# Seven block products in the first product of chunk 0, and two blocks of W2 converted during the attention

## The chip, the cores and the metric

One core of one Trainium2 chip runs the whole program. Time is the device time of one execution in microseconds (us). In this text TensorE makes matrix products and transposes, VectorE, ScalarE and GpSimd (POOL) work on elements, and SP (SyncE) issues the DMA transfers.

## The reference

```python
def reference(**kwargs):
    ...
    attn_out = _attn_ref(**attn_kwargs)      # sliding window of 64, (4, 8, 576, 64)
    x = np.ascontiguousarray(attn_out.transpose(0, 2, 1, 3)).reshape(B, S, H * D)
    x = _moe_ref(x=x, **moe_kwargs)
    return _moe2_ref(x=x, **moe2_kwargs)

def _moe_ref(x, w_in, w_spatial, b_spatial, w_out):
    h = np.maximum(x @ w_in, 0.0)
    u, v = (h[..., :512], h[..., 512:])
    ...                                      # v_n: v normalised over its last axis
    v_s = np.einsum('ts,bsd->btd', w_spatial, v_n) + b_spatial[None, :, None]
    return ((u * v_s) @ w_out)

def _moe2_ref(x, w_tok1, w_tok2, w_ch1, w_ch2):
    h = np.maximum(x.transpose(0, 2, 1) @ w_tok1, 0.0) @ w_tok2
    u = x + h.transpose(0, 2, 1)
    h2 = np.maximum(u @ w_ch1, 0.0) @ w_ch2  # 512 -> 1536 -> 512
    return (u + h2)
```

There are 4 x 576 = 2304 tokens of 512 features. The weights come as float64. In what follows W1 is `w_ch1` and W2 is `w_ch2`.

## The kernel before

Every large product is made of three matmuls: each factor is split into a rounded high part and a low part (h and l at the end of a name), and high x high, high x low and low x high are added (`mm3`, line 161). A split is a cast on ScalarE (line 148) and a subtraction on VectorE or POOL (line 149). A float64 weight is first made float32 out of its two 32-bit words: `down` on ScalarE (line 72), then `to_f32` on VectorE (lines 63, 68, 69). This whole step is called a conversion below.

The program has three stages. The first is the attention with the first half of the MoE block. It runs in 18 turns whose instructions are in an order written out by hand (`manual_schedule`, lines 463 to 565). A turn n transposes the softmax of turn n (line 285), takes the exponentials of turn n+1 (line 264) and their norm (`rs`, lines 272 to 274), and makes the scores and the maximum of turn n+2 (lines 241 and 255). Between them run pieces of the MoE block's products as work to fill TensorE, among them the spatial product, whose PSUM bank VectorE empties in lines 394 and 395. SP loads q and k (`qq`, `kk`) three turns ahead and v (`va`, `vb`) two turns ahead. All transfers of the kernel stand in SP's one queue, in program order.

The second stage makes, per piece, `wout` (the product with w_out), `x2nat` (transposes), `tok1` and `tok2` (the two products over tokens), and beside them converts the weights of the channel MLP. `load_c1(j)`, j = 0 to 5, converts two column tiles of W1, splits them, forms four sums of their blocks on POOL and stores these to DRAM (`sums`, line 717). `load_c2(j)` converts two row tiles of W2, forms block sums on POOL (line 738), splits all eight blocks (the low part on POOL, line 149) and stores them to DRAM (`scr`, line 742). Here the order on each engine is a list scheduler's; the conversions are given a later priority (`later`, LATER). Their raw words, their float32 values and their high and low parts live in a ring of eight buffers of 4 KB a partition (`k4`). `tok1` splits its result with `hl` on VectorE (line 672); `tok2` needs that `hl`.

The third stage goes over the tokens in three chunks of 768. The first product of a chunk (512 to 1536) goes over six block rows j. Chunk 0 makes it plainly: `ch1` (line 819) for column tiles j and j+6. Chunks 1 and 2 make it by `ch1_seven` (line 838): a two-by-two block product with seven products in place of eight. That needs sums of the activations' blocks, t1 to t4 (`usums`, split into spare places), and the sums of W1, loaded back (`load_sums`). The second product is `product` (line 889): seven block products with weights loaded from `scr`; it is the same in all chunks.

Of the kernel before, what the change touches and what calls it, by code (L numbers as in the profile page):

```python
# [35 lines left out]
def tile_kernel(ctx, tc, qT, kT, kE, v, w_in, wsT, b_sp, w_out, w_t1, w_t2, w_c1, w_c2, outT):  # L36
# [422 lines left out]
    def wv_part(k):  # L459
        return w_part(U[:, k, 1152:2176], w_in[128 * k:128 * k + 128, 512:].unsqueeze(1), wi_h[:, k:k + 1, 512:], wi_l[:, k:k + 1, 512:], 512)  # L460

    E = mybir.EngineType
    with tc.manual_schedule(engines={E.PE, E.SP, E.Activation, E.DVE, E.Pool}):
# [61 lines left out]
        uv_v(*its[0])  # L525
        conv, late = {1: (0,), 2: (1, 2), 3: (3,)}, ()
        ws_at = {2: 2, 3: 2, 4: 3, 5: 3}
        for n in range(1, len(its)):
            more, some = n + 2 < len(its), n + 1 < len(its)
            cv = [wu[i] for i in conv.get(n, ())]  # L530
            if n > 1:
                if n + 3 < len(its):
                    load_qk(n + 3)
                if more:
                    load_v(n + 2)
            PT = att_turn(n, busy={1: 2, 2: 8}.get(n, 0))
# [12 lines left out]
            go(*cv[1:])
            att_pv(n, PT)  # L550
            go(*cv[1:])
            if more:
                scores(n + 2)
                smax(n + 2, 0)
                smax(n + 2, 1)
            if n > 1:
                tick()
            late = cv[1:]
            while work and left > 0:
                left -= run_work(1)  # L560
# [166 lines left out]
    @later  # L727
    def load_c2(j):

        X = [k4() for _ in range(2)]  # L730
        Y = [x.rearrange("p (s c) -> p s c", s=4) for x in X]
        convert(X[0])

        def blk(s, n=1):
            return Y[s // 4][:, s % 4:s % 4 + n, :]

        for o, a, b, op in ((4, 1, 3, ALU.add), (5, 4, 0, ALU.subtract), (6, 0, 1, ALU.subtract), (7, 2, 5, ALU.subtract)):
# [16 lines left out]
    def usums(c, u):  # L754

        t0 = TW * c
        (uh, ul), (vh, vl) = u
        x11, x21, x12, x22 = [U[:, k:k + 2, t0 + h:t0 + h + HW] for h in (0, HW) for k in (0, 2)]

        def thirds(t):  # L760
            return t.rearrange("p k (j c) -> p k j c", c=128)

        def apart(w, words):
            v = words.rearrange("p (j w r k c) -> p j w r k c", j=3, w=2, r=2, k=4)
            return v[:, :, w, 1, :2].rearrange("p j k c -> p k j c")
# [16 lines left out]
    tok1(0)  # L782
    load_c2(1)
    x2nat(1)
    wout(3)
    tok2(0)
    load_c2(2)
    load_c1(1)
# [16 lines left out]
    tok1(3)  # L805
    load_c2(4)
    tok2(2)
    u = [uin(0, 0)]
    load_c1(4)
    tok2(3)  # L810
# [7 lines left out]

    def ch1(u, ft):

        out = []
        for uh, ul in u:
            ps = psmm.tile([P, 512], F32, tag="mm", name="mm")[:, :HW]
# [13 lines left out]

    def ch1_seven(X):

        x11, x21, x22, t1, t2, t3, t4 = X  # L840
        S = [load_sums(j) for j in range(2)]
        outs, left = [], []
        for j in range(NJ):
            if j and j + 1 < NJ:
                S.append(load_sums(j + 1))
            s1, s2, s3, s4 = S[j]
            a, c = [psmm.tile([P, 512], F32, tag="mm", name="mm")[:, :HW] for _ in range(2)]
# [64 lines left out]
    for c in range(NTOK // TW):  # L912
        t0 = TW * c
        u = u[:1] if c == 0 else []
        u += [uin(c, h) for h in range(len(u), 2)]
        if c:
            b11, b12, b21, b22, e = ch1_seven(usums(c, u))
        else:
            b11, b12, b21, b22, e = [], [], [], [], []
            for j in range(NJ):  # L920
                if j == 0:
                    load_c1(5)
                    load_c2(5)
                x, y = ch1(u, j)
                b11.append(x)
                b12.append(y)
                x, y = ch1(u, j + NJ)
                b21.append(x)
                b22.append(y)
                e.append(diff(H(), b12[j], b11[j], nc.vector))  # L930
                diff(b12[j], b22[j], b12[j], nc.vector)
        us = [[U[:, 2 * dh:2 * dh + 2, t0 + HW * h:t0 + HW * h + HW] for h in range(2)] for dh in range(2)]
# [119 lines left out]
```

## Time and profile before

| | |
|---|---|
| median of 3 runs | 638.13 us (638.07 to 638.38) |
| profiled execution, its own time | 638.47 us |
| its span | 636.7 us |
| TensorE busy | 610.3 us, 96%, 4455 matmuls and transposes |
| VectorE busy | 459.5 us, 72% |
| ScalarE busy | 334.1 us, 52% |
| POOL busy | 153.4 us, 24% |
| TensorE's granted clock | 1.00 over nearly the whole span |
| DMA | 103.60 MB, mean 163 GB/s |

The profile is of one execution; the span is from its first to its last instruction, and the program's own time is a little longer. The attention ends near 215 us. The stage of wout, tok1 and tok2 runs to 363.5, chunk 0 from there to about 500 (its first product to 412), and chunks 1 and 2 follow, each started a little before the one ahead of it ends. A line of a timeline gives start, busy time, engine, source line and tiles; in square brackets stands the idle time of the engine just before it and what ended it.

### The profile page before, as it was taken

Reading aid. Unit: us, or ns where it says so; the run is one execution under the profiler, and the core shown is the slowest. Engines: PE = TensorE matmul, PEld = TensorE weight load, DVE = VectorE, ACT = ScalarE, POOL = GpSimd, SP = SyncE. Lnnn points to the kernel's source line nnn. Section 1 sums busy time; section 2 is a strip of 40 time slices with the busy share of each in tenths; the row PEclk is TensorE's granted clock in tenths of the full one; section 3 lists DMA queues with packets and bytes.
Section 4 is the critical chain, followed back from the end, with each engine's and each line's share of the span. In section 5 each row is a group of like instructions: output and inputs, shape, how many; then the busy total and the mean of one; then the engine's idle time right before and its main releaser. Section 6 shows DMA issues by size and latency. Waiting matters only on the chain.

```text
span 636.7 us, 12004 instructions
## 1 busy us (share of the span) xinstructions
PE 610.3 (96%) x4455; PEld 566.8 (89%) x4455; DVE 459.5 (72%) x977; ACT 334.1 (52%) x839; POOL 153.4 (24%) x166
## 2 busy tenths in 40 slices
PE   5889999999999999999899999999999999999997
PEld 2568798998889899888788899999999999999987
DVE  4896857556584688769978951278875998867982
ACT  4777853545674464666554442345543646344550
POOL 5610000100010010565475471041000440002510
PEclk9999999999999999999999999999999999999999
DMA  8853473222330135557756455057433675534772
GB/s 325 271 158 112 152 235 127 78 77 75 102 116 2 34 118 158 177 193 248 256 183 218 183 174 218 0 198 257 149 125 133 220 230 196 178 103 151 255 248 75
DMA packets 46106, 103.60 MB, mean 163 GB/s; under 512 B 4192, under 2 KB 16736, under 8 KB 46048
## 3 DMA queue, kind: packets, MB, share of 16 engines
q1 hardware_dynamic: 46048, 102.84, 48.3%
q8 instruction: 35, 0.57, 0.4%
q14 instruction: 23, 0.19, 0.1%
HBM read 83.95 MB, written 18.87 MB: 162 GB/s over the span
## 4 chain that ended last, share of the span: by engine, by line
PE 64%; DVE 14%; ACT 7%; DMA 5%; issue 4%; POOL 3%; SPq 1%; DVEq 0%; ACTq 0%; POOLq 0%
PE mm L161 27%; PE A L904 17%; PE mm L833 8%; PE A L833 6%; ACT pb L264 3%; DMA U<-in_w_in 3%; POOL k L738 2%; DVE k L68 2%; DVE k L69 2%; PE xo L297 2%; PE pt L285 2%; DMA scr<-hl 2%; DVE k L63 1%; PE A L161 1%; PE sc L241 1%
## 5 line engine op out<-in xcount | busy, mean ns | idle before, releaser
L904 PE MATMUL A<-oh,w 128*128 128x384 f32 x480 | 102.7, 334 | 0.0
L886 POOL TENSOR_TENSOR H<-H 128x384 f32<-128x384 f32 x36 | 45.0, 1264 | 184.9 <-DVE ol L899 171.0
L899 DVE TENSOR_TENSOR ol<-H,oh 128x384 fp32r<-128x384 f32 x120 | 77.2, 676 | 16.4 <-ACT oh L898 12.7
L904 PEld LDWEIGHTS A<-oh,w 128*128 128x128 f32 x480 | 85.0, 188 | 0.0
L898 ACT CAST oh<-H 128x384 fp32r<-128x384 f32 x120 | 60.0, 514 | 41.5 <-PE A L904 31.0
L904 PE MATMUL A<-ol,w 128*128 128x384 f32 x240 | 61.4, 336 | 2.2 <-DVE ol L899 2.2
L161 PE MATMUL mm<-ws,nh 128*128 128x288 f32 x320 | 62.0, 297 | 0.4 <-DVE tmp L394 0.4
L161 PEld LDWEIGHTS mm<-ws,nh 128*128 128x128 f32 x320 | 49.9, 188 | 1.0 <-DVE tmp L394 0.6
L363 POOL TENSOR_SCALAR rstd<-mv 128x1 f32<-128x1 f32 x18 | 4.9, 272 | 178.4 <-DVE mv L362 178.3
L904 PEld LDWEIGHTS A<-ol,w 128*128 128x128 f32 x240 | 43.1, 188 | 3.3 <-DVE ol L899 3.2
L886 DVE TENSOR_TENSOR H<-H 128x384 f32<-128x384 f32 x36 | 22.6, 628 | 21.8 <-ACT H L826 19.6
L161 PE MATMUL mm<-ws,nl 128*128 128x288 f32 x128 | 37.7, 295 | 0.0
L264 ACT ACTIVATE pb<-pb,nm 128x128 f32<-128x128 f32 x96 | 37.3, 400 | 0.4 <-DVE nm L255 0.4
L286 ACT COPY PT<-pt 128x512 f32<-128x512 f32 x36 | 19.4, 591 | 31.5 <-PE pt L285 31.5
L272 DVE TENSOR_SCALAR rs<-sm 128x8 f32<-128x8 f32 (+1 forms) x19 | 3.3, 172 | 42.9 <-ACT pb L264 42.9
L161 PE MATMUL mm<-xh,wi_h 128*128 128x384 f32 x96 | 32.7, 341 | 0.7 <-ACT vf L357 0.6
L161 PE MATMUL mm<-xh,wi_l 128*128 128x384 f32 x96 | 32.1, 334 | 0.0
L161 PE MATMUL mm<-xl,wi_h 128*128 128x384 f32 x96 | 32.1, 334 | 0.0
L161 PE MATMUL mm<-gh,wo_h 128*128 128x512 f32 (+1 forms) x80 | 29.4, 378 | 0.1
L161 PE MATMUL mm<-gh,wo_l 128*128 128x512 f32 (+1 forms) x80 | 29.4, 370 | 0.0
L161 PE MATMUL mm<-gl,wo_h 128*128 128x512 f32 (+1 forms) x80 | 29.4, 370 | 0.0
L149 POOL TENSOR_TENSOR hl<-k,hl 128x512 fp32r<-128x512 f32 (+1 forms) x24 | 28.6, 1208 | 0.0
(190 smaller groups left out, 1691.4 us busy)
## 6 DMA issues: line engine op xcount, KB each, us to landing
w<-scr SPq DMA_DIRECT2D x63, 512.0 KB, 4.4
k<-in_w_c SPq DMA_DIRECT2D x24, 512.0 KB, 5.3
scr<-hl SPq DMA_DIRECT2D x18, 512.0 KB, 6.1
kk<-in_kT SPq DMA_DIRECT2D x16, 384.0 KB, 4.7
k<-sums SPq DMA_DIRECT2D x12, 512.0 KB, 3.2
qq<-in_qT SPq DMA_DIRECT2D x18, 256.0 KB, 4.0
va<-in_v SPq DMA_DIRECT2D x18, 256.0 KB, 2.9
vb<-in_v SPq DMA_DIRECT2D x18, 256.0 KB, 3.9
```

What stands on the lines that cost most here:

```text
L68: nc.vector.scalar_tensor_tensor(out=y, in0=high, scalar=-0x80000000, in1=y, op0=ALU.bitwise_and, op1=ALU.bitwise_or)
L69: nc.vector.scalar_tensor_tensor(out=y, in0=low, scalar=29, in1=y, op0=ALU.logical_shift_right, op1=ALU.bitwise_or)
L149: eng.tensor_tensor(out=lo, in0=x, in1=f(hi), op=ALU.subtract)
L161: nc.tensor.matmul(o, a, c, start=(i == 0), stop=(i == n - 1))
L264: nc.scalar.activation(out=pb[:, h, :], in_=scs[g][:, h - 4 * g, :] if mk is None else pb[:, h, :], func=AF.Exp, scale=SCALE if mk is None ...
L285: nc.tensor.transpose(pt[:, h, :], pb[:, 4 * g + h, :], ident)
L286: nc.scalar.copy(out=PT[:, 4 * g:4 * g + 4, :], in_=pt)
L833: nc.tensor.matmul(o, a, m, start=first and i == 0, stop=i == len(todo) - 1, skip_group_check=True)
L886: eng.tensor_tensor(out=out, in0=a, in1=b, op=ALU.subtract)
L898: nc.scalar.copy(out=oh, in_=blk[j])
L899: nc.vector.tensor_tensor(out=ol, in0=blk[j], in1=f(oh), op=ALU.subtract)
L904: nc.tensor.matmul(acc[d], a, m, start=(first and j == 0 and i == 0), stop=(last and j == NJ - 1 and i == 2), skip_group_check=True)
```

## The change

In the first product of chunk 0 only block rows 0 and 1 are made plainly; rows 3, 4, 5 and 2, in that order, are made by seven block products as in the other chunks. So t1 to t4 and the sums of W1 are needed for chunk 0 too, and `usums` gives them in two steps, one after the first plain row and one after the second, into other spare places. And W2's blocks j = 0 and 1 are converted during the attention by `early_c2`, in the same manner as `load_c2` but with the four sums and the low parts on VectorE and in free columns of the tile U: block 0 in turns 2 to 6, block 1 in turns 6 to 10. Each is a generator whose steps (load, downs, to_f32, sums, casts, subtractions, stores) are called at one of three points of a turn: before the exponentials ("exp"), after the scores ("mid"), and at the end ("end"). The other ten conversions keep their functions; their order of loads changes, and load_c2(4) and (5) are called in the two plain rows.

```diff
+    def early_c2(j):
...
+        for r, src in zip(raw, c2_source(j)):
+            nc.sync.dma_start(out=r, in_=src.bitcast(I32))
...
+        yield
+        for i, (low, high) in enumerate(parts):
+            down(span(2, 2 * i, 2), high)
+        yield
+        to_f32(span(2, 0, 4), parts)
+        yield
+        for o, a, b, op in C2_SUMS:
+            nc.vector.tensor_tensor(out=val[o], in0=val[a], in1=val[b], op=op)
+        yield
+        homes = ((2, 2, 0, 0, 2), (4, 2, 0, 2, 2), (6, 2, 1, 0, 2), (0, 1, 1, 2, 1))
+        for s, n, r, at, w in homes:
+            nc.scalar.copy(out=span(r, at, n).bitcast(F32R), in_=span(2 + s // 4, s % 4, n))
+        yield
+        for s, n, r, at, w in homes:
+            x = span(2 + s // 4, s % 4, n)
+            nc.vector.tensor_tensor(out=x.bitcast(F32R), in0=x, in1=span(r, at, n), op=ALU.subtract)
+        yield
+        for h, blocks in ((0, ((2, 4, 0, 0), (6, 2, 1, 0), (0, 1, 1, 2))), (1, ((4, 4, 3, 0), (2, 2, 2, 2), (0, 1, 2, 0)))):
+            for s, n, r, at in blocks:
+                nc.sync.dma_start(out=scr[s:s + n, j // 2, :, j % 2, h].rearrange("s p c -> p s c"), in_=span(r, at, n).rearrange("p (s c) -> p s c", c=256))
...
+        EARLY, FROM = 2, 2
+        side = [early_c2(j) for j in range(EARLY)]
+        at = {(FROM + 4 * j + t, point): side[j] for j in range(EARLY)
+              for t, point in ((0, "end"), (1, "mid"), (2, "exp"), (3, "exp"), (3, "mid"), (4, "exp"), (4, "mid"))}
...
-                ((2, 0), (1, 0), (2, 1), (2, 2), (1, 1), (1, 2), (2, 3), (1, 3), (2, 4), (1, 4), (1, 5), (2, 5))]
+                ((1, 0), (2, 2), (1, 1), (1, 2), (2, 3), (1, 3), (1, 4), (1, 5), (2, 4), (2, 5))]
...
-        for i, o, a, b in ((0, t1, x12, x11), (1, t2, x22, t1), (2, t3, x22, x12), (3, t4, x21, t2)):
+        for i, o, a, b in ((0, t1, x12, x11), (1, t2, x22, t1)):
             nc.vector.tensor_tensor(out=o, in0=a, in1=b, op=ALU.subtract)
             split(*homes[i], thirds(o))
...
+        yield
+        for i, o, a, b in ((2, t3, x22, x12), (3, t4, x21, t2)):
+            nc.vector.tensor_tensor(out=o, in0=a, in1=b, op=ALU.subtract)
+            split(*homes[i], thirds(o))
...
+    def ch1_all(u, parts, plain):
+
+        outs, left = {}, []
+        seven_js = [j for j in (*range(NJ // 2, NJ), *range(NJ // 2))] if plain else list(range(NJ))
+        seven_js = [j for j in seven_js if j >= plain]
+        for j in range(plain):
+            if j < 2:
+                load_c2(4 + j)
+            outs[j] = ch1_four(u, j)
+            if j == 0:
+                next(parts)
...
+        S = {j: load_sums(j) for j in seven_js[:2]}
+        x11, x21, x22, t1, t2, t3, t4 = next(parts)
+        for at, j in enumerate(seven_js):
+            if at and at + 1 < len(seven_js):
+                S[seven_js[at + 1]] = load_sums(seven_js[at + 1])
+            s1, s2, s3, s4 = S.pop(j)
...
+        b11, b12, b21, b22, e = ch1_all(u, usums(c, u), 0 if c else 2)
```

Three places where the order moves. The first is SP's queue at the end of turn 6 and the start of turn 7; this is a piece of the difference. The first two rows end the loads of v for turn 8, the last two are q and k of turn 10.

```order
 L215 DMA va<-in_v 128x512
 L216 DMA vb<-in_v 128x512
+L508 DMA scr<-U 128x4x256
+L508 DMA scr<-U 128x2x256
+L508 DMA scr<-U 128x256
+L508 DMA scr<-U 128x4x256
+L508 DMA scr<-U 128x2x256
+L508 DMA scr<-U 128x256
+L486 DMA U<-in_w_c 128x1024 x2
 L200 DMA qq<-in_qT 128x512
 L203 DMA kk<-in_kT 128x768
```

Six stores of block 0 and two loads of block 1 now stand between the two. Behind `kk` come three raw pieces of w_out (line 85), as before.

The second place is VectorE near the end of the second stage, around the two `hl` of tok1(1). Before (the conversion with k4_4303 is c1(3)):

```order
L149 TENSOR_TENSOR ul_4459<-U_83,uh_4458 128x768 x2
L335 TENSOR_TENSOR nl_4042<-A_4036,nh_4041 128x512
L343 TENSOR_TENSOR nh_4050<-A_4045,nh_4050 64x512
L672 SCALAR_TENSOR_TENSOR hl_4102<-A_4086,hh_4101 128x512
L63 TENSOR_SCALAR k4_4303<-k4_4303 128x1024
L68 SCALAR_TENSOR_TENSOR k4_4303<-k4_4133,k4_4303 128x512
L68 SCALAR_TENSOR_TENSOR k4_4303<-k4_4135,k4_4303 128x512
L672 SCALAR_TENSOR_TENSOR hl_4121<-A_4105,hh_4120 128x512
```

And with the change (line 672 is now 729; k4_4291, k4_4349 and k4_4439 are c1(3), c1(4) and c1(5), k4_4544 is c2(4)):

```order
L149 TENSOR_TENSOR ul_4434<-U_83,uh_4433 128x768 x2
L149 TENSOR_TENSOR c1b_4067<-k4_4291,c1b_4067 128x1024
L149 TENSOR_TENSOR c1b_4067<-k4_4349,c1b_4067 128x1024
L343 TENSOR_TENSOR nh_4038<-A_4033,nh_4038 64x512
L149 TENSOR_TENSOR c1b_4067<-k4_4439,c1b_4067 128x1024
L63 TENSOR_SCALAR k4_4544<-k4_4544 128x1024
L729 SCALAR_TENSOR_TENSOR hl_4090<-A_4074,hh_4089 128x512
L729 SCALAR_TENSOR_TENSOR hl_4109<-A_4093,hh_4108 128x512
```

The ninth conversion now begins before both `hl`, and three splits of W1 stand there as well.

The third place is TensorE at the start of chunk 0's first product, with the change. `mm_4592` is the second of the first two plain sums, `th` holds t2 and `sh` a sum of W1; line 891 is the product of a seventh, line 161 a plain one.

```order
L161 MATMUL mm_4592<-ul_4434,ws_98 128x384
L161 MATMUL mm_4592<-uh_4433,ws_98 128x384 x2
L161 MATMUL mm_4592<-ul_4434,ws_98 128x384
L161 MATMUL mm_4592<-uh_4433,ws_98 128x384
L891 MATMUL A_4764<-th_4640,sh_4746 128x384
L891 MATMUL A_4827<-th_4640,sh_4752 128x384
L161 MATMUL mm_4607<-uh_4538,ws_98 128x384
L161 MATMUL mm_4622<-uh_4538,ws_98 128x384
```

Before, all of chunk 0's first product is of line 161. Now one matmul each of rows 3 and 4 stands behind the first 24 plain ones.

## Rows read from the trace of the kernel before

**Rows 1.** The page, section 1: busy time of engines, share of the span, instructions.
```profile
span 636.7 us, 12004 instructions
PE 610.3 (96%) x4455; PEld 566.8 (89%) x4455; DVE 459.5 (72%) x977; ACT 334.1 (52%) x839; POOL 153.4 (24%) x166
```
**Rows 2.** Table by stretch; its first line names the columns.
```profile
core 0: us, PE busy (x) PEld busy (x) DVE busy (x) ACT busy (x) POOL busy (x), PEclk, DMA share, GB/s
290.00:363.50 73.50, 69.77 (x428) 62.08 (x426) 65.72 (x104) 38.42 (x68) 42.30 (x44) 1.00 0.61 215
363.50:412.00 48.50, 48.47 (x279) 48.44 (x280) 16.01 (x24) 17.26 (x35) 14.97 (x13) 1.00 0.38 136
455.00:500.00 45.00, 45.00 (x262) 45.00 (x261) 32.79 (x54) 21.02 (x38) 3.52 (x3) 1.00 0.42 144
500.00:512.00 12.00, 11.24 (x66) 10.92 (x64) 12.00 (x19) 5.66 (x14) 4.20 (x3) 1.00 0.74 252
```
**Rows 3.** The chain that ended last, 360 to 420: start, us, engine, line, count.
```profile
363.53 48.17 PE mm L161 x276
411.70 4.16 PE A L904 x24
```
**Rows 4.** Timeline of turns 4 and 5: VectorE's rs, TensorE's transposes.
```profile
62.45 0.17 DVE L272 TENSOR_SCALAR rs<-sm 128x8 f32<-128x8 f32 x1 [3.29 <-ACT pb L264]
69.17 0.17 DVE L272 TENSOR_SCALAR rs<-sm 128x8 f32<-128x8 f32 x1 [0.78 <-ACT pb L264]
...
70.99 1.07 PE L285 MATMUL pt<-ident,pb 128*128 128x128 f32 x8 [0.80 <-ACT ws L101]
```
**Rows 5.** Timeline of VectorE, two operations of 128x256.
```profile
306.74 0.75 DVE L642 TENSOR_TENSOR gl<-U,gh 128x256 fp32r<-128x256 f32 x2
```
**Rows 6.** Timeline of SP, an issue at the end of turn 6.
```profile
79.38 0.54 SPq L200 DMA_DIRECT2D qq<-in_qT  x1
```
**Rows 7.** Table by stretch in turn 7, and the page's DMA issues (KB each, us to landing).
```profile
82.00:87.00 5.00, 5.00 (x36) 4.97 (x35) 2.02 (x8) 3.00 (x11) 0.00 (x0) 1.00 0.93 320
93.00:98.00 5.00, 4.92 (x38) 4.68 (x36) 5.00 (x26) 0.00 (x0) 0.00 (x0) 1.00 0.77 255
...
scr<-hl SPq DMA_DIRECT2D x18, 512.0 KB, 6.1
```
**Rows 8.** Timeline of turn 7: ScalarE, VectorE and TensorE.
```profile
90.99 0.78 ACT L72 ACTIVATE val<-raw 128x256 f32<-128x256 f32 x2
...
95.48 0.69 DVE L312 TENSOR_TENSOR xl<-xo,xh 128x512 fp32r<-128x512 f32 x1
...
97.77 0.46 DVE L394 TENSOR_TENSOR tmp<-mm,bb 128x288 f32<-128x288 f32 x1
...
98.28 0.53 PE L161 MATMUL mm<-ws,nh 128*128 128x288 f32 x2 [0.36 <-DVE tmp L394]
```
**Rows 9.** Timeline of VectorE: conversions c2(0), c1(0), c2(1), c1(3) and c2(5).
```profile
254.51 0.69 DVE L63 TENSOR_SCALAR k<-k 128x1024 int32<-128x1024 int32 x1 [1.04 <-ACT k L72]
266.18 1.19 DVE L63 TENSOR_SCALAR k<-k 128x1024 int32<-128x1024 int32 x1 [4.41 <-ACT k L72]
275.10 0.68 DVE L63 TENSOR_SCALAR k<-k 128x1024 int32<-128x1024 int32 x1
...
326.73 1.69 DVE L63 TENSOR_SCALAR k<-k 128x1024 int32<-128x1024 int32 x1 [1.30 <-ACT k L72]
328.45 1.29 DVE L68 SCALAR_TENSOR_TENSOR k<-k,k 128x512 int32<-128x512 int32 x2
...
363.76 1.23 DVE L63 TENSOR_SCALAR k<-k 128x1024 int32<-128x1024 int32 x1
```
**Rows 10.** Timeline of TensorE in tok2(1): the first matmuls that need each hl.
```profile
326.47 0.29 PE L161 MATMUL mm<-t_h,hl 128*128 128x288 f32 x1
...
330.40 0.40 PE L161 MATMUL mm<-t_h,hl 128*128 128x288 f32 x1 [0.72 <-DVE hl L672]
```

More of the change, by code (lines that the diff above doesn't have):

```diff
@@ L460, in wv_part, with c2_source, span @@
         return w_part(U[:, k, 1152:2176], w_in[128 * k:128 * k + 128, 512:].unsqueeze(1), wi_h[:, k:k + 1, 512:], wi_l[:, k:k + 1, 512:], 512)
+    HW, TW, NJ = 384, 768, 6
+    scr = tc.dram_tile([8, NJ // 2, P, 2, 2, 256], F32, name="scr")
+    def c2_source(j):
+        return [w_c2[128 * r:128 * r + 128, :] for r in (j, j + NJ)]
+    C2_SUMS = ((4, 1, 3, ALU.add), (5, 4, 0, ALU.subtract), (6, 0, 1, ALU.subtract), (7, 2, 5, ALU.subtract))
+    def early_c2(j):
+        raw, hi, val = [], [], []
+        for k in range(4):
+            home = U[:, k, 1152:2176]
+            if k < 2:
+                raw.append(home.bitcast(I32))
+                hi += [home.bitcast(F32R)[:, 256 * i:256 * i + 256] for i in range(4)]
+            else:
+                val += [home[:, 256 * i:256 * i + 256] for i in range(4)]
+        def span(r, at, n):
+            return U[:, r, 1152 + 256 * at:1152 + 256 * at + 256 * n]
+        parts = []
+        for r, src in zip(raw, c2_source(j)):
+            nc.sync.dma_start(out=r, in_=src.bitcast(I32))
+            r3 = r.rearrange("p (n w) -> p n w", w=2)
+            parts.append((r3[:, :, 0], r3[:, :, 1]))
+        yield
[18 more added lines that the diff above has]
+                nc.sync.dma_start(out=scr[s:s + n, j // 2, :, j % 2, h].rearrange("s p c -> p s c"), in_=span(r, at, n).rearrange("p (s c) -> p s c", c=256))
     E = mybir.EngineType
@@ L526, in tile_kernel, with beside @@
         conv, late = {1: (0,), 2: (1, 2), 3: (3,)}, ()
+        EARLY, FROM = 2, 2
+        side = [early_c2(j) for j in range(EARLY)]
+        at = {(FROM + 4 * j + t, point): side[j] for j in range(EARLY)
+              for t, point in ((0, "end"), (1, "mid"), (2, "exp"), (3, "exp"), (3, "mid"), (4, "exp"), (4, "mid"))}
+        def beside(n, point):
+            if (n, point) in at:
+                next(at[n, point], 0)
         ws_at = {2: 2, 3: 2, 4: 3, 5: 3}
@@ L535, in tile_kernel @@
                     load_v(n + 2)
+            beside(n, "start")
             PT = att_turn(n, busy={1: 2, 2: 8}.get(n, 0))
@@ L540, in tile_kernel @@
             go(*cv[:1])
+            beside(n, "exp")
             if some:
@@ L557, in tile_kernel @@
                 tick()
+            beside(n, "mid")
             late = cv[1:]
@@ L562, in tile_kernel @@
             load_ws(ws_at.get(n, 0))
+            beside(n, "end")
             enable(n)
@@ L735, in blk @@
             return Y[s // 4][:, s % 4:s % 4 + n, :]
-        for o, a, b, op in ((4, 1, 3, ALU.add), (5, 4, 0, ALU.subtract), (6, 0, 1, ALU.subtract), (7, 2, 5, ALU.subtract)):
+        for o, a, b, op in C2_SUMS:
             nc.gpsimd.tensor_tensor(out=blk(o), in0=blk(a), in1=blk(b), op=op)
@@ L782, in tile_kernel @@
     tok1(0)
-    load_c2(1)
+    load_c2(2)
     x2nat(1)
@@ L786, in tile_kernel @@
     tok2(0)
-    load_c2(2)
     load_c1(1)
@@ L805, in tile_kernel @@
     tok1(3)
-    load_c2(4)
+    load_c1(4)
     tok2(2)
     u = [uin(0, 0)]
-    load_c1(4)
+    load_c1(5)
     tok2(3)
@@ L817, in tile_kernel, with ch1 @@
     Hp = pool("Hp", "right", stack=c_stack, bufs=1)
-    def ch1(u, ft):
+    def ch1(u, j):
         out = []
-        for uh, ul in u:
+        for (uh, ul), ft in [(x, ft) for x in u for ft in (j, j + NJ)]:
             ps = psmm.tile([P, 512], F32, tag="mm", name="mm")[:, :HW]
@@ L836, in H, with ch1_four @@
         return Hp.tile([P, HW], F32, tag="H", name="H", bufs=30)
[L838 to L846, printed above, removed]
+    def ch1_four(u, j):
+        x, z, y, w = ch1(u, j)
+        e = diff(H(), y, x, nc.vector)
+        return x, diff(y, w, y, nc.vector), z, w, e
+    def ch1_all(u, parts, plain):
[8 more added lines that the diff above has]
+                next(parts)
+        if not plain:
+            next(parts)
+        S = {j: load_sums(j) for j in seven_js[:2]}
[4 more added lines that the diff above has]
+            s1, s2, s3, s4 = S.pop(j)
             a, c = [psmm.tile([P, 512], F32, tag="mm", name="mm")[:, :HW] for _ in range(2)]
@@ L880, in ch1_seven @@
             left = [last]
-            outs.append((h11, h12, h21, h22, e))
+            outs[j] = (h11, h12, h21, h22, e)
         left[0]()
-        return [list(x) for x in zip(*outs)]
+        return [list(x) for x in zip(*(outs[j] for j in range(NJ)))]
     def diff(out, a, b, eng=nc.gpsimd):
@@ L915, in tile_kernel @@
         u += [uin(c, h) for h in range(len(u), 2)]
[L916 to L931, printed above, removed]
+        b11, b12, b21, b22, e = ch1_all(u, usums(c, u), 0 if c else 2)
         us = [[U[:, 2 * dh:2 * dh + 2, t0 + HW * h:t0 + HW * h + HW] for h in range(2)] for dh in range(2)]
```

11 lines of the change are left out of this document (3 added, 8 removed).

## The prediction

> **What bounds the kernel now.** I read the page's busy line first: TensorE is busy 610.3 of 636.7 us, 96%, and no other engine is over 72% [rows 1]. So time goes only by fewer matmuls or by less of TensorE's 26.4 us of idle, and time comes only by new idle there. The table by stretch says where idle is left: 3.7 us in the stage after the attention (290 to 363.5: 69.77 busy of 73.50), none to speak of in the first product of chunk 0 (48.47 of 48.50), none where chunk 1 makes the same product by seven block products (45.00 of 45.00), 0.8 in the 12 us in which VectorE is full and chunk 2 is made ready (500 to 512: VectorE 12.00, TensorE 11.24) [rows 2]. The chain that ended last then gives a matmul's price: through chunk 0 it runs on TensorE alone, and 24 matmuls of 128x384 take 4.16 us, 0.173 us each [rows 3]. Last I read each place that the change touches for the idle time in front of its instructions.
>
> The profiled execution took 638.47 us, its span is 636.7, so 1.77 lie around it; the median of the runs is 638.13, 0.34 less. The sum is made on 638.47 and 0.34 taken off. What a measurement of this kernel can tell from no change is 0.2%, here 1.28 us: faster means under 636.85, slower over 639.41.
>
> **Part 1: fewer matmuls.** A block row costs 48 matmuls plainly (two weight tiles, two halves of 384 tokens, four k, three products of the split) and 42 by seven products. Four rows change: 4 x 6 = 24 matmuls fewer, 24 x 0.173 = 4.16 us off a path without idle. That is the whole gain in matmuls.
>
> **Part 2: what the seven products need in time.** The subtractions t1, t2 and their splits come from the place where chunk 1's come, and the first matmuls of rows j=3 and j=4 stand behind only 24 plain matmuls, 4.2 us, in TensorE's order. They need t2 split and the sums of both rows loaded, whose stores end a W1 conversion. The nearest row for a like preparation is the 0.8 us of 500 to 512 [rows 2]; below nothing it can't be, since the stretch has no idle to give back, and above it is bounded by the 4.2 us between plain row and seventh product. VectorE has room: it works 16.01 of 48.50 there [rows 2]. I take the lower half, +0.5, near to the row that shows it (0 to 4.2).
>
> **Part 3: two W2 blocks in the attention.** Per block VectorE gets a to_f32 of one 128x1024 and four 128x512, four sums of 128x256 and four subtractions; ScalarE two downs and four casts; SP two loads of 512 KB and six stores of 1,792 KB together. By turn:
> - to_f32, turn 4: the 128x1024 takes 0.69 at its shortest and two L68 of 128x512 take 1.29 [rows 9], two L69 as much: 3.27 us, and VectorE sits idle 3.29 us before the turn's first rs [rows 4]. Hidden; were that idle gone, the softmax of the turn would be up to 3.3 us late and TensorE with it.
> - sums, turn 5: two 128x256 took 0.75 [rows 5], four take 1.5; before that turn's rs only 0.78 is idle, and TensorE waits at this turn's transposes already, 0.80 [rows 4]. So +0.7 (0, if the sums slip beside a wait, to 1.5).
> - casts, subtractions (turns 5 and 6) and block 1 in turns 8 to 10: they stand before rs's with slack or in turns where TensorE has other work; nothing (up to 0.5, inside the range).
> - stores of block 0 and loads of block 1 at the end of turn 6: SP's order has all eight between v(8) and qq(10). Behind them on SP stand qq and kk of turn 10, whose scores come two turns later, and w_out's raw pieces, which VectorE waits for at once. Bytes from SP's 79.38 on [rows 6] to the first of them (a tile of 128x512 is 256 KB): qq, kk 768 KB, v 512, stores 1,792, loads 1,024, qq, kk 640, one piece 256: 4,992 KB = 5.11 MB. The stretch 82 to 87 moved 320 GB/s at a share of 0.93 [rows 7], which is 344 at a full one. From 80 that is 14.9 us at 344, 16.0 at 320: the piece lands at 94.9 to 96.0. ScalarE's down takes 0.39 (0.78 for two [rows 8]). VectorE now has this L63 ahead of an L395, the split xl, the smax of the next turn, an L68, a second L63 and the L394 that frees a bank of PSUM for the spatial product. Before, xl to that L394 ran from 95.48 to 97.77 [rows 8], 2.3; the L63s, L395 and L68 add about 1.1: 3.4. So L394 would start at 98.7 to 99.8 in place of 97.77, and TensorE, which waited 0.36 for it at 98.28 [rows 8], stops 0.9 to 2.0 longer. I take +1.5. Bounds: at the 255 GB/s of 93 to 98 [rows 7] the bytes take 20.0 us, which makes +6; below, nothing, since TensorE's wait is no more than 0.36.
>
> The page's own row for such a store is 512 KB in 6.1 us to landing [rows 7], slower than the full share, but several overlap. The Trainium skill ("DMA: Bandwidth & Descriptors", Bandwidth) measured 341 GB/s for one transfer of 1 MB and 425 for 16 MB. By the first the sum stays; by the second the bytes take 12.0 us, the L394 is not late and the term is 0, which makes 635.2. The fullest stretch of this trace [rows 7] stands by the first.
>
> **Part 4: two conversions fewer after the attention.** VectorE, ScalarE and POOL lose two of twelve in that stage. TensorE has only 3.7 us of idle to give back there [rows 2]: -3.7 at the best. Against that the order moves. VectorE's L63 of c2(4) now stands before both hl splits of tok1(1), where before the first hl stood before c1(3)'s L63 and the second behind it. If each conversion keeps its pace, 11.67 us after a W2 block (254.51 to 266.18) and 8.92 after a W1 block (266.18 to 275.10) [rows 9], then the ninth, with two of W2 and six of W1 ahead, starts at 254.51 + 2 x 11.67 + 6 x 8.92 = 331.4. (These two paces give 366.4 for the last L63, which stood at 363.76, so they are a little long.) The first hl would end 1.4 later, 332.8, and its first matmul stood at 326.47 [rows 10]: 6.3 late, less the 0.72 that TensorE waits there now [rows 10], +5.6. But a pace is no speed: VectorE waits 4.41 us for ScalarE at 266.18 [rows 9], the ring of buffers holds up W2 blocks more than W1 blocks, and with two of them gone the ninth comes sooner. Following each queue by hand I come to 328 for the first hl, one us late. Between -3.7 and +5.6 I take 0: one us lost at hl, about one won of the 3.7 that the trace shows.
>
> **The sum.** 638.47 - 4.16 + 0.5 + 0.7 + 1.5 + 0 = 637.0 for a profiled execution; less 0.34: **636.7**.
>
> **Rivals.**
> - The forecast, 636.7, own range 635.4 to 637.9: chance 0.42, of it 0.24 under 636.85.
> - The stage after the attention gives all its idle back: with two conversions fewer the waits there go, -3.7, so 633.0. For it: VectorE and POOL are near their fill there (65.72 and 42.30 of 73.50 [rows 2]). Against: the hl splits move behind a conversion. Chance 0.21.
> - The transfer block of turn 6 to 7 costs twice my term: at 300 GB/s the piece lands at 97.0, the L394 starts at 100.8, +3.0 in place of 1.5, 638.2. For it: the stores are pieces of 1 KB and wait for the last subtractions of block 0. Against: TensorE may have scores to make meanwhile. Chance 0.16, no change.
> - The slower side: c2(4) before hl. TensorE's second product tok2(1) waits for hl behind a conversion that isn't ready, +5.6 in place of 0, so 642.3; +4 if the pace is the little shorter one that the last L63 tells. It decides from the point where c2(4)'s L63 starts later than 325.1 (326.47 less 1.4) on TensorE's clock; from 327.8 on it costs 2.7, and the time is over the bound. For it: the paces. Against: VectorE had 4.41 us of idle in front of single conversions. Chance 0.18.
> - The rest (the seven products of row 4 late by up to the 4.2 us; the change doing nothing, because the sums are loaded late): 0.03, slower.
>
> **How the numbers follow.** Faster: 0.24 + 0.21 = 0.45. Within 0.2%: 0.18 + 0.16 = 0.34. Slower: 0.18 + 0.03 = 0.21. The range leaves out the best of the second case (the idle and the wait at turn 7 both gone, 631.5) and the worst of the fourth: 632.8 to 641.0.
>
> **What would show it.** Right: TensorE has 24 matmuls fewer (4431); the stretch of chunk 0's first product is 44.3 to 44.9 us and shows under 1 us of idle; the transposes of turn 6 wait about 0.7 us longer; one wait of 1 to 2.5 us for L394 stands near 98 us; the stage from 290 on keeps 3 to 5 us of idle. Wrong in the gain: under 2 us of idle in that stage. Wrong to the slower side: a single wait of TensorE for hl (L729 now) of over 3 us, with an L63 of 128x1024 right before it on VectorE, itself waiting for ScalarE's down; or a wait for L394 of over 4 us at turn 7. Wrong in the sums: a wait at the first seven-product matmuls, released by a load of sums.

## The result, and the profile after

The changed kernel takes 643.62 us (median of 5, 642.66 to 644.77) against 638.38 before (638.07 to 638.53): 1.0081 times as long, interval 1.0067 to 1.0095. It is slower by 5.2 us where 636.7 was forecast; the range ended at 641.0. Its profiled execution took 643.63 us, its span is 641.9.

The page after, sections 1 and 2 (the granted clock in 40 equal slices):

```profile
span 641.9 us, 12034 instructions
PE 610.2 (95%) x4431; PEld 566.4 (88%) x4431; DVE 490.2 (76%) x1025; ACT 341.6 (53%) x851; POOL 136.9 (21%) x150
PEclk9999997999999999999999999999999999999999
```

TensorE has the 24 matmuls fewer (4431 for 4455 [rows 1]), worth 4.2 us, and yet is as long busy as before. One slice of the clock, from 96 to 112 us, reads 7: there, and once more behind 335 us (below), the work that was left out was paid back by matmuls at a lower clock. The table by stretch shows where idle came:

```profile
core 0: us, PE busy (x) PEld busy (x) DVE busy (x) ACT busy (x) POOL busy (x), PEclk, DMA share, GB/s
60.00:100.00 40.00, 35.54 (x425) 32.19 (x423) 31.32 (x116) 28.19 (x100) 2.38 (x6) 1.00 0.75 254
100.00:215.00 115.00, 112.42 (x1113) 103.68 (x1114) 76.49 (x260) 60.25 (x215) 7.13 (x18) 0.97 0.29 93
290.00:363.50 73.50, 68.35 (x401) 60.26 (x400) 61.03 (x97) 39.50 (x71) 40.70 (x40) 0.98 0.53 188
363.50:412.00 48.50, 48.50 (x292) 48.50 (x291) 27.79 (x46) 21.11 (x37) 0.00 (x0) 1.00 0.30 101
```

Idle in 290 to 363.5 went from 3.7 us [rows 2] to 5.2 (the work in it now comes some 5.6 us later), and the clock's mean is under 1.00 in two stretches. Three marks on TensorE's timeline cut the span into stages that can be compared between kernels: the two unused matmuls (line 283) just ahead of the transposes of turn 1, where the written-out turns begin to repeat, the transposes of the last turn, 17, and the first plain matmul of chunk 0. Turns are counted from 0.

| kernel | attention, turn 1 to turn 17 | to chunk 0 | from there to the end |
|---|---|---|---|
| before | 25.05 to 208.78: 183.73 | to 360.57: 151.79 | to 636.7: 276.13 |
| after | 24.71 to 214.34: 189.63 (+5.90) | to 369.27: 154.93 (+3.14) | to 641.9: 272.63 (-3.50) |

The three differences and the start, 0.34 earlier, make the 5.2 us of the spans.

**Turn 7.** SP, ScalarE, VectorE and TensorE in the timeline after (a view each, one turn):

```profile
81.50 5.31 SPq L508 DMA_DIRECT2D scr<-U  x6
87.63 1.40 SPq L486 DMA_DIRECT2D U<-in_w_c  x2
...
90.02 1.45 SPq L85 DMA_DIRECT2D raw<-in_w_out  x3
...
96.73 0.43 ACT L72 ACTIVATE val<-raw 128x256 f32<-128x256 f32 x1 [2.19 <-DMA raw<-in_w_out]
...
97.19 0.29 DVE L63 TENSOR_SCALAR val<-val 128x256 int32<-128x256 int32 x1 [2.91 <-ACT val L72]
...
100.60 0.45 DVE L394 TENSOR_TENSOR tmp<-mm,bb 128x288 f32<-128x288 f32 x1
...
101.10 0.85 PE L161 MATMUL mm<-ws,nh 128*128 128x288 f32 x2 [2.93 <-DVE tmp L394]
```

Read from the end: TensorE waits 2.93 us (0.36 before [rows 8]) for a bank that L394 frees; L394 stands behind L63, which waits for ScalarE's down, which waits for w_out's piece, which was issued behind stores and loads. The piece goes out at 90.02 where it went out at 86.90 before, and takes 6.7 us to land where it took 3.1. The first line below is the time from SP's `qq`, from which the prediction counts its bytes, to the piece's landing: the DMA engines are busy throughout (share 0.99), at 335 GB/s. The others show the clock.

```profile
79.49:96.71 17.22, 17.22 (x169) 16.79 (x169) 9.40 (x32) 9.57 (x33) 0.79 (x2) 1.00 0.99 335
...
98.00:100.00 2.00, 0.17 (x2) 0.00 (x0) 2.00 (x16) 0.00 (x0) 0.00 (x0) 1.00 0.85 335
100.00:102.00 2.00, 0.90 (x4) 0.90 (x5) 2.00 (x8) 0.00 (x0) 0.00 (x0) 0.58 0.03 11
102.00:104.00 2.00, 2.00 (x10) 2.00 (x10) 1.97 (x6) 0.00 (x0) 0.00 (x0) 0.50 0.59 143
104.00:106.00 2.00, 2.00 (x11) 1.98 (x10) 1.11 (x4) 0.28 (x1) 0.00 (x0) 0.50 0.33 119
106.00:108.00 2.00, 2.00 (x13) 2.00 (x12) 1.93 (x4) 1.73 (x7) 0.00 (x0) 0.72 0.00 0
```

From the end of the idle stretch TensorE runs at the lower of its two levels, 1.2 of 2.4 GHz, until about 107 us: 10 matmuls in 2 us where 17 to 19 fit.

**The hl of tok1(1).** VectorE, then POOL, then TensorE:

```profile
327.98 2.88 DVE L149 TENSOR_TENSOR c1b<-k,c1b 128x1024 fp32r<-128x1024 f32 x2
330.89 0.69 DVE L343 TENSOR_TENSOR nh<-A,nh 64x512 fp32r<-64x512 f32 x1
331.62 1.61 DVE L149 TENSOR_TENSOR c1b<-k,c1b 128x1024 fp32r<-128x1024 f32 x1
333.15 1.21 DVE L63 TENSOR_SCALAR k<-k 128x1024 int32<-128x1024 int32 x1
334.39 1.29 DVE L729 SCALAR_TENSOR_TENSOR hl<-A,hh 128x512 fp32r<-128x512 f32 x2
...
328.04 3.42 POOL L772 TENSOR_TENSOR k<-k 128x256 f32<-128x256 f32 x2 [2.87 <-DMA sums<-k]
331.42 2.39 POOL L772 TENSOR_TENSOR k<-k,k 128x256 f32<-128x256 f32 x2
...
335.14 0.40 PE L161 MATMUL mm<-t_h,hl 128*128 128x288 f32 x1 [2.97 <-DVE hl L729]
```

TensorE waits 2.97 us for hl (0.72, and for the second one only, before [rows 10]). The L63 of c2(4) stands right before it, as the slower rival had it, but no row of VectorE has idle in brackets: the L63 waits for nothing. VectorE is simply behind, with three splits of W1 in a row. Those rows are also longer than elsewhere: the three L149 and the L63 take 5.7 us beside POOL's sums of W1, where the same forms take 1.22 each (the split `sl` of this kernel) and 0.68, 4.3 together. The stretch behind it again has a lower clock: 335 to 340 shows 0.66.

### The profile page after: what moved, and what is told of

It reads as the page before. It is cut to its first block, busy times and chain, and to the rows that moved or that the text cites. A ratio compares the mean times of both kernels' runs of the same rounds, so it can differ in the third digit from the quotient of the medians.

```text
span 641.9 us, 12034 instructions
## 1 busy us (share of the span) xinstructions
PE 610.2 (95%) x4431; PEld 566.4 (88%) x4431; DVE 490.2 (76%) x1025; ACT 341.6 (53%) x851; POOL 136.9 (21%) x150
## 4 chain that ended last, share of the span: by engine, by line
PE 66%; DVE 15%; DMA 6%; ACT 6%; issue 4%; SPq 1%; POOL 1%; DVEq 0%; ACTq 0%; POOLq 0%
PE mm L161 23%; PE A L978 17%; PE mm L891 10%; PE A L891 8%; PE A L161 4%; ACT pb L264 2%; PE xo L297 2%; PE pt L285 2%; DMA k<-in_w_c 2%; DVE gl L699 1%; DVE k L69 1%; DVE pb L274 1%; DMA U<-in_w_in 1%; PE sc L241 1%; DVE k L68 1%
## 5 line engine op out<-in xcount | busy, mean ns | idle before, releaser
L960 POOL TENSOR_TENSOR H<-H 128x384 f32<-128x384 f32 x36 | 43.4, 1224 | 208.3 <-DVE ol L973 154.0
L161 PE MATMUL mm<-ws,nh 128*128 128x288 f32 x320 | 63.9, 303 | 2.9 <-DVE tmp L394 2.9
L978 PE MATMUL A<-ol,w 128*128 128x384 f32 x240 | 63.0, 337 | 2.7 <-DVE ol L973 2.7
L161 PEld LDWEIGHTS mm<-ws,nh 128*128 128x128 f32 x320 | 51.5, 194 | 3.6 <-DVE tmp L394 3.2
L960 DVE TENSOR_TENSOR H<-H 128x384 f32<-128x384 f32 x36 | 23.9, 664 | 9.3 <-ACT H L941 4.7
L941 ACT ACTIVATE H<-H 128x384 f32<-128x384 f32 x32 | 16.4, 525 | 24.8 <-DVE H L940 24.8
L995 DVE TENSOR_TENSOR U<-A,U 128x384 f32<-128x384 f32 x42 | 21.9, 550 | 8.7 <-PE A L978 4.3
```

The lines of the kernel that those rows point to most:

```text
L161: nc.tensor.matmul(o, a, c, start=(i == 0), stop=(i == n - 1))
L941: nc.scalar.activation(out=o, in_=o, func=AF.Relu)
L960: eng.tensor_tensor(out=out, in0=a, in1=b, op=ALU.subtract)
L978: nc.tensor.matmul(acc[d], a, m, start=(first and j == 0 and i == 0), stop=(last and j == NJ - 1 and i == 2), skip_group_check=True)
L995: nc.vector.tensor_tensor(out=at, in0=src, in1=at, op=ALU.add)
```

## The experiments

Each was timed in 4 to 12 runs beside the kernel before on the same chip; the ratio is to that. Not all ran on the same chip, so kernels are compared by their ratios and by the stages of one profiled execution each (differences are to the kernel before). By the timed runs only e2 (slower) and e8 to e11 (faster) stand clear of the kernel after; the intervals of the others overlap its own, and what they tell is read from their traces. The last columns hold TensorE's longest wait for L394 in turn 7 and for an hl of tok1(1). Where the clock fell in a wait or right behind it, a c stands beside it.

| kernel | ratio (interval) | attention | to chunk 0 | rest | L394 | hl |
|---|---|---|---|---|---|---|
| before | | 183.73 | 151.79 | 276.13 | 0.36 | 0.72 |
| after | 1.0081 (1.0067 to 1.0095) | +5.90 | +3.14 | -3.50 | 2.93 c | 2.97 c |
| e1 seven products alone | 1.0057 (1.0037 to 1.0076) | -0.06 | -0.43 | +3.74 | 0.33 | 0.70 |
| e2 early conversions alone | 1.0149 (1.0122 to 1.0176) | +5.16 | +2.27 | +0.09 | 3.32 c | 2.96 c |
| e3 block 1 one turn later | 1.0058 (1.0039 to 1.0078) | +2.74 | +3.49 | -3.57 | 1.12 and 0.98 | 2.97 c |
| e4 filler in the wait | 1.0065 (1.0042 to 1.0088) | +4.57 | +3.28 | -3.57 | filled | 2.97 c |
| e5 low parts on POOL | 1.0094 (1.0067 to 1.0122) | +3.17 | +4.35 | -3.56 | 2.94 | none |
| e6 old order of conversions | 1.0055 (1.0035 to 1.0075) | +6.10 | +1.55 | -3.38 | 3.10 c | 1.52 |
| e7 all one turn earlier | 1.0109 (1.0084 to 1.0133) | +7.09 | +1.11 | -3.34 | 0.37 | 2.97 |
| e8 stores after w_out | 0.9996 (0.9986 to 1.0006) | +0.67 | +3.27 | -3.49 | 0.34 | 2.96 c |
| e9 e8 and old order | 0.9984 (0.9973 to 0.9994) | +0.66 | +1.30 | -3.42 | 0.34 | 1.20 |
| e10 e9, c1(3) low on POOL | 1.0002 (0.9985 to 1.0019) | +0.73 | +2.74 | -3.37 | 0.38 | 1.77 c |
| e11 e10, sums on POOL | 0.9984 (0.9971 to 0.9998) | +0.37 | +1.42 | -3.44 | 0.38 | 1.63 |

**e1, the seven products alone.**

```diff
-        EARLY, FROM = 2, 2
+        EARLY, FROM = 0, 2
...
-                ((1, 0), (2, 2), (1, 1), (1, 2), (2, 3), (1, 3), (1, 4), (1, 5), (2, 4), (2, 5))]
+                ((2, 0), (1, 0), (2, 1), (2, 2), (1, 1), (1, 2), (2, 3), (1, 3), (1, 4), (1, 5), (2, 4), (2, 5))]
...
```

> Only the seven products in chunk 0; W2's blocks 0 and 1 are converted after the attention as before, so all twelve conversions stand there. Theory (the 5.6 us in turns 5 to 8 come from the early conversions, the 3.1 us after the attention from VectorE, which has more to do before the hl of tok1(1)): the attention is as before, chunk 0 gains 3.5 us, and the stage after the attention loses at least as much as now: 638.4 - 3.5 + 3 to 5 = 638 to 640. Rival (the loss after the attention comes with the early conversions too, by their order of loads): 634.9.

641.69 us against 637.74. The attention is as before, so its loss is the early conversions' alone. But the stage after the attention lost nothing; the loss stands in chunk 0, and the theory's reason for it was wrong. TensorE, timeline of chunk 0:

```profile
380.21 0.45 PE L893 MATMUL mm<-uh,c1b 128*128 128x384 f32 x1 [1.53 <-ACT p L929]
383.13 0.69 PE L893 MATMUL A<-th,sh 128*128 128x384 f32 x1 [1.57 <-ACT sh L148]
```

With twelve conversions behind the attention the sums of W1 come too late: their split `sh` is what one of the seven products waits for. SP issues their first load at 378.22, behind six stores of W2 blocks, where the kernel after issues it at 358.29. In these waits the clock falls as well (0.65 and 0.50 in the two stretches of 2 us from 382 to 386). The matmuls saved are lost again, 3.74 us over. The early conversions are what makes the seven products pay: in every kernel that has both, this stage gains 3.3 to 3.6.

**e2, the early conversions alone.**

```diff
         outs, left = {}, []
+        if plain:
+            for j in range(NJ):
+                if j < 2:
+                    load_c2(4 + j)
+                outs[j] = ch1_four(u, j)
+            return [list(x) for x in zip(*(outs[j] for j in range(NJ)))]
```

> Only the early conversions; chunk 0 is made plainly, with the other ten conversions in the changed order of loads. Theory: turns 5 to 8 cost 5.6 us as in the changed kernel, and the wait for hl after the attention stays, since the same conversions stand ahead of it: 638.4 + 5.6 + 2 to 3 = 646 to 647. Rival (two conversions fewer give that stage its 3.7 us of idle back once chunk 0 asks for no sums): 638.4 + 5.6 - 3.7 = 640.3.

647.46 against 637.74, 9.7 us more (interval 1.22% to 1.76%, 7.8 to 11.2); 646 to 647 from 638.4 was 7.6 to 8.6. The profiled execution is one of the shorter ones (646.06), and its stages explain 7.5. The wait for hl is 2.96 though nothing in chunk 0 asks for sums: it belongs to the conversions' order. Two conversions fewer gave no idle back.

**e3, block 1 one turn later.**

```diff
-        at = {(FROM + 4 * j + t, point): side[j] for j in range(EARLY)
+        at = {(FROM + 5 * j + t, point): side[j] for j in range(EARLY)
```

> The changed kernel with every step of block 1 one turn later, so that its two loads (1 MB) stand behind w_out's raw pieces on SP in turn 7; the six stores of block 0 stay ahead of them. Theory (VectorE waits 2.9 us for the piece of w_out, TensorE then for L394, and after that its clock is halved for some 6 us): the piece lands 1.05 MB at 390 GB/s, 2.7 us, earlier, the wait of 2.9 us falls under 0.5 and the clock stays at 1.00: 643.6 - 5 = 638.6. Rival (the six stores or VectorE's order alone make the wait): 643, with a wait for L394 of over 2 us.

641.99 against 637.74, 4.3 us more where the kernel after takes 5.2 more: by the timed runs 1 us of the 5 expected, with intervals that overlap. In the profiled execution the attention is 3.2 us shorter. TensorE's timeline of turn 7:

```profile
96.11 0.54 PE L161 MATMUL mm<-ws,nh 128*128 128x288 f32 x2 [1.12 <-DVE tmp L394]
101.08 0.53 PE L161 MATMUL mm<-ws,nh 128*128 128x288 f32 x2 [0.98 <-DVE tmp L394]
```

One long wait became two of 1 us and the clock stayed in this turn. From the transposes of turn 7 to those of turn 9 it is 29.30 us, 2.0 over before, where the kernel after is 5.3 over. So the loads ahead of w_out's piece are worth 3.3; the six stores, still ahead of it, the rest, which e8 takes away.

**e4, the filler.**

```diff
+            if (b, d, c0) == (0, 2, 288):
+                keep_busy(12, psa.tile([P, 512], F32, tag="xo", name="xo", bufs=1))
             ps = psmm.tile([P, 512], F32, tag="mm", name="mm")
```

> The changed kernel with twelve matmuls of 128x512 in bf16 that nobody uses, into the bank of xo, ahead of the spatial half that waits for L394 in turn 7; xo's bank is free only after its split, about 0.3 us into the wait. Theory (the halved clock after the wait is half of the cost): the wait stays, 2.9 us, but the clock is 1.00 from 98 to 108: 643.6 - 3 = 640.6. Rival (the clock falls for another reason, or the filler delays more than it keeps): 643.6 or above.

642.29 against 637.74. The timed ratios of e4 and of the kernel after overlap, so the runs alone don't decide it; the trace speaks for it. In its execution w_out's piece came later, at 98.50 on ScalarE, and TensorE's stop to the next half lasted from about 98.6 to 102.87; the filler stands in it:

```profile
100.27 2.75 PE L188 MATMUL xo<-ident 128*128 128x512 bf16 x12 [1.66 <-DVE xl L312]
102.87 0.53 PE L161 MATMUL mm<-ws,nh 128*128 128x288 f32 x2
```

The clock reads 1.00 in every 2 us from 94 to 110, and the attention is 1.33 shorter than after's although this stop is over a microsecond longer. That the filler kept the clock is not shown by one execution: in e5, below, it stayed without one.

**e5, low parts on POOL.**

```diff
-        split(both[:, :1024], both[:, 1024:], x)
+        split(both[:, :1024], both[:, 1024:], x, nc.vector if j < 3 else nc.gpsimd)
```

> The changed kernel with the low parts of W1's blocks 3 to 5 on POOL in place of VectorE: three L149 of 128x1024, 1.4 to 1.6 us each, leave the row of VectorE's work that ends with the two hl of tok1(1); nothing else moves. Theory (hl is late because VectorE is full there, not because one conversion waits): hl starts some 4.5 us earlier, TensorE's wait of 2.97 us for it falls under 0.5 and the clock stays at 1.00 after it, 3.0 + 1.7 us: 643.6 - 4.5 = 639.1, less what POOL's longer row costs later. Rival (hl waits behind the L63 of c2(4), which waits for its words): the wait stays near 3 and the time near 643.6.

644.83 against 638.28 (641.25 to 647.08; its profiled execution is the shortest of them). The wait for hl is gone, as the theory had it, but the time isn't: POOL's three splits slow VectorE. VectorE, then POOL:

```profile
330.21 5.09 DVE L69 SCALAR_TENSOR_TENSOR k<-k,k 128x512 int32<-128x512 int32 x2
...
329.11 5.65 POOL L149 TENSOR_TENSOR c1b<-k,c1b 128x1024 fp32r<-128x1024 f32 x2
```

Two L69 that take 1.28 us alone take 5.09 beside them, and three waits of 1.00 to 1.57 follow between 335 and 347; behind the last the clock falls (0.61 and 0.54 in the two stretches of 2 us from 348). The Trainium skill ("SBUF — State Buffer", SBUF: two separate sides) describes this as a port that VectorE and GpSimd share and that one of them holds for its whole instruction; this row agrees, with 2.5 us for one L69 and 2.8 for one of POOL's subtractions.

This kernel and e6 also show the clock's price. Both stop in turn 7 for about 3 us. Table by stretch of e5:

```profile
98.00:100.00 2.00, 0.00 (x0) 0.00 (x0) 2.00 (x17) 0.00 (x0) 0.00 (x0) 1.00 0.21 81
102.00:104.00 2.00, 2.00 (x19) 2.00 (x18) 1.93 (x6) 1.08 (x3) 0.00 (x0) 1.00 0.60 186
```

and of e6:

```profile
98.00:100.00 2.00, 0.00 (x0) 0.00 (x0) 2.00 (x17) 0.00 (x0) 0.00 (x0) 0.86 0.26 104
102.00:104.00 2.00, 2.00 (x10) 1.99 (x9) 1.17 (x3) 0.00 (x0) 0.00 (x0) 0.50 0.67 195
```

From the end of the wait to the transposes of turn 9, the same work, it is 100.32 to 114.65 = 14.33 us in e5 and 100.30 to 117.36 = 17.06 in e6; in the kernel after 101.10 to 118.17 = 17.07. The fallen clock costs 2.7 us, and after the same wait (2.94 and 3.10) it fell in one and not in the other.

**e6, the old order of conversions.**

```diff
-                ((1, 0), (2, 2), (1, 1), (1, 2), (2, 3), (1, 3), (1, 4), (1, 5), (2, 4), (2, 5))]
+                ((1, 0), (2, 2), (1, 1), (1, 2), (2, 3), (1, 3), (2, 4), (1, 4), (1, 5), (2, 5))]
...
-            if j < 2:
-                load_c2(4 + j)
+            if j == 0:
+                load_c1(5)
+                load_c2(5)
```

> The changed kernel with the ten conversions in the order that they had before (c2(4) before c1(4), c1(5) and c2(5) last, these two called in the first plain row). Theory (the order, three W1 blocks in a row, fills VectorE ahead of hl): only one split of W1 stands ahead of hl, its wait falls from 2.97 to under 1, the clock stays: -4 us; but the sums of row 5 come one conversion later, 0 to 3 us of waits at the first seventh products: 640 to 642.5. Rival (it is the number of conversions or the seven products, not the order): wait near 3, 643.6.

642.46 against 638.28. With one split of W1 ahead of hl in place of three the wait is 1.52, the clock stays there, and the stage is 1.55 over before's instead of 3.14. The sums still come in time (-3.38). The theory's direction holds for the wait, its size (a wait under 1) doesn't. And the 1.6 us that the stage gains can't be put down to the shorter wait itself: e7, below, has the full wait of 2.97 with the clock at 1.00 behind it, and its stage is 1.11 over, less than here. What is shorter here at hl returns later (waits of 0.74 and 0.49 before chunk 0).

**e7, all one turn earlier** (`FROM = 1`).

> The changed kernel with every step of both blocks one turn earlier (block 0 in turns 1 to 5, block 1 in 5 to 9), so that the six stores and the two loads stand on SP about 14 us before w_out's raw pieces. Theory (turn 7's loss is the transfers ahead of w_out's piece, and the halved clock after the wait): no wait for L394 over 0.5 us, clock 1.00 at 98 to 108, turn 8 starts within 1 us of the kernel before: 643.6 - 5 = 638.6; the subtractions in turn 5, 2.2 us against 0.78 of idle, may cost 1.4 there. Rival (VectorE's longer row in turn 7, not the transfers): a wait near 2 us stays, 642.

645.25 against 638.28. The wait for L394 is as before (0.37): the bytes were its cause. But turns 3 to 6 have no room: the transposes of turns 5 and 6 wait 1.96 and 2.04 for the softmax, behind the second of these waits the clock falls (0.50 from 76 to 78, 0.67 to 80), and the attention is the longest of all. The step gave back in one place what it took in another. It tells one thing more: here the clock stayed 1.00 after a wait of 2.97 for hl, and from that wait's end to chunk 0 it is 32.57 us, 1.56 less than after's 34.13.

**e8, the stores after w_out's pieces.**

```diff
-        at = {(FROM + 4 * j + t, point): side[j] for j in range(EARLY)
-              for t, point in ((0, "end"), (1, "mid"), (2, "exp"), (3, "exp"), (3, "mid"), (4, "exp"), (4, "mid"))}
+        at = {(FROM + 5 * j + t, point): side[j] for j in range(EARLY)
+              for t, point in ((0, "end"), (1, "mid"), (2, "exp"), (3, "exp"), (3, "mid"), (4, "exp"), (5, "exp") if j == 0 else (4, "mid"))}
```

> The changed kernel with block 0's six stores in turn 7 before the exponentials, behind w_out's first raw pieces on SP, and every step of block 1 one turn later. Theory (turn 7's loss is the bytes ahead of w_out's piece): no wait for L394 above 0.5 us and no halved clock in turn 7, turn 8 starts within 1 us of the kernel before: 643.6 - 5 = 638.6; the wait for hl stays near 3. Rival (the early conversions load VectorE too much in any place): a wait of 1 us or more near turn 7 or 8 stays, 641 or more.

638.05 against 638.37, no difference: 5 us of the loss are gone with an edit that moves stores and steps alone. TensorE's timeline, turn 7 and hl:

```profile
98.51 0.53 PE L161 MATMUL mm<-ws,nh 128*128 128x288 f32 x2 [0.34 <-DVE tmp L394]
...
328.80 0.61 PE L161 MATMUL mm<-t_h,hl 128*128 128x288 f32 x1 [2.96 <-DVE hl L729]
```

The attention is 0.67 over before's, which is turn 5's sums; the wait for hl is untouched.

**e9, both orders** (e8 with e6's order).

> The kernel with the stores after w_out's pieces and block 1 one turn later, and the ten conversions in the order of before. Both theories together: turn 7 as before, the wait for hl about 1.5 and its stage 1.6 us longer than before, the seven products 3.5 us shorter, turn 5 0.6 longer: 638.4 + 0.6 + 1.6 - 3.5 = 637. Rival (the losses return elsewhere): 639 or more.

637.28 against 638.37: 0.9984, interval 0.9973 to 0.9994, so faster than both kernels, if by 1.1 us only, which is less than the 0.2% that the prediction counted as a change. The terms came as expected: 0.66, 1.30 and -3.42. The mean granted clock of each timed run is known too: seven of the twelve here have 0.999 or 1.00, in e8 one of twelve, in the kernel after none of five (0.989 to 0.995). So the clock falls less often with this order.

**e10, c1(3)'s low part on POOL too.**

```diff
-        split(both[:, :1024], both[:, 1024:], x)
+        split(both[:, :1024], both[:, 1024:], x, nc.gpsimd if j in (3,) else nc.vector)
```

> As the kernel with both changes of order, and the low part of W1's block 3 on POOL: one L149 of 1.4 us less ahead of the hl of tok1(1). Theory (VectorE's row ahead of hl is what TensorE waits for): the wait for hl falls from about 1.5 to under 0.5, and with it the chance of a halved clock: 636. Rival (POOL's later sums bring a wait of the same size behind it): 637 or more.

638.10 against 638.37: a miss. The wait for hl rose to 1.77, and the clock fell behind it, so the stage lost 2.74. With one L149 less VectorE stands idle for 0.97 us before the L63 of c2(4), which waits for ScalarE's downs, and hl starts at 326.73 where it started at 326.79 in e9. In this shorter row the slower rival's mechanism is there after all.

**e11, the sums on POOL.**

```diff
-            nc.vector.tensor_tensor(out=val[o], in0=val[a], in1=val[b], op=op)
+            nc.gpsimd.tensor_tensor(out=val[o], in0=val[a], in1=val[b], op=op)
```

> As the kernel before this one, and the four sums of each early block on POOL in place of VectorE (POOL has 7 us of work in the 115 us from 100 to 215). Theory (turn 5's 0.6 us are the sums ahead of rs): the transposes of turn 6 start as in the kernel before: 635.4. Rival (POOL's sums come too late for the casts, or slow VectorE): 636 or more.

637.27 against 638.37, as e9. The attention's loss falls from 0.7 to 0.37, half of what the sums were thought to cost; 635.4 was not reached, since the hl part of e10 doesn't pay.

## Why the prediction was wrong

- **Fewer matmuls and the start of the seven products** (-4.16 + 0.5 = -3.66): right. -3.50 after, and -3.3 to -3.6 in every kernel with both parts.
- **Turn 5's sums** (+0.7): right. The transposes of turn 6 come 0.62 later, counted from the first mark. The other steps cost nothing, as taken: from the transposes of turn 9 to those of the last turn it is 96.17 us before and after.
- **The transfer block in turn 7** (+1.5): the mechanism was right at each link, the term mis-sized, and its second half missing. The wait grew by 2.6, not 1.5: at 344 GB/s w_out's piece would have landed at 94.9, it came near 96.7, 17.2 us behind SP's 79.49; for the 5.11 MB counted that is 297 GB/s, the third rival's rate. But the rate was not what failed: in that time the DMA engines moved 335 GB/s, near the 344 taken, and so 5.8 MB. The count was 0.7 MB short; which other transfers moved beside the piece is not shown one by one. The larger part is what no term named: the clock fell in the wait, 2.7 us. Together 5.3 where 1.5 stood, which is turns 7 and 8 to a tenth. e8 undoes this by moving the bytes, e3 undoes 3.3 of it, e7 all of it in that place.
- **The stage after the attention** (0, between -3.7 and +5.6): this is the step that failed in sign. It lost 3.14. The queues followed by hand gave 328 for the first hl; on the clock of the kernel before (5.56 us less, by which the last turn is late) its first matmul stands at 329.6, and the c2(4) conversion's L63 at 327.6. The fourth rival had the place, hl, and the price to within its range, but not the reason: c2(4) did not wait for its words. W1 blocks had taken the places of W2 blocks, and a W1 block leaves its split with VectorE where a W2 block leaves it with POOL; so VectorE was full, and e5 and e6 take the wait away or halve it by taking that work off. The wait is not the whole price: with the clock at 1.00 the stage loses 1.1 to 1.55 (e6, e7, e9, e11), with a fall behind hl 2.3 to 3.5 (after, e2, e3, e4, e8, e10). So about half of the 3.14 is the clock again, and the other half no run took away. The gain side (-3.7) was not there: e2, with two conversions fewer and nothing else asked, lost 2.27 in this stage.
- The profiled execution lies 6.6 us above the sum, 643.63 for 637.0: 3.8 of it come from turn 7 and 3.1 from this stage. The two waits were weighed as rivals with their own prices and taken in the forecast near their lower ends both; they came together. Each was made longer in its effect by the clock, which was in no term and no bound. For the same reason no sign of being slower was met, a wait of over 4 us for L394 or of over 3 for hl: the waits were 2.93 and 2.97, and the rest of the loss shows as busy time, not as idle.

What stays open: why the clock falls after one wait and not after another. It fell in or right behind waits of 1.5 to 3.3 us (the shortest are two of 1.53 and 1.57 close together in e1, and one of 1.57 in e5) and stayed behind some of 1.52, 1.63, 1.96, 2.94 and 2.97. The runs show that both occur, not what decides. It explains the spread of 3 to 6 us in the times of several kernels only in part: in e5 the three runs with a mean clock of 0.997 took 641.25 to 644.30 us and the two with 0.992 took 646.19 and 647.08, but in e4 the longest run, 644.63, has 0.997.

## What to carry to other kernels

A transfer that looks free because its queue has room must be counted against what is issued behind it in the same queue and which in-order engine will stand still for that: here 2.9 MB put ahead of one small piece cost 5.3 us, and putting them behind it cost nothing. A wait on TensorE of about 3 us should be priced at up to twice its length, as the clock may be low behind it, and that part shows as busy time. And where work is moved out of a stage, count each engine's part of what takes its place, since the number of steps can fall while the fullest engine gets more.

## What was not expected of the hardware

In or right behind idle of 1.5 to 3.3 us TensorE's clock fell to half for some microseconds in some executions (in the kernel after TensorE works at half from 101 to 107), at a price of 1.6 to 2.7 us where it can be compared, and stayed at 1.00 in others. VectorE's operations on 128x512 with two inputs were four times as long (5.09 us for 1.28) beside POOL's subtractions. And some eight transfers queued together moved 377 and 408 GB/s in the two stretches of 2 us from 94 to 98, more than the 344 that the kernel before let one expect; over the 17.2 us that counted it was 335.
